# Attention and token/channel mixer on one core: the last tokens of all batches as a ninth batch, seeded banks, heads in pairs, order from a table

## The chip, the cores and the metric

The kernel runs on one core of a Trainium2 chip. The core has TensorE (PE; its weight loads are PEld), VectorE (DVE), ScalarE (ACT), GpSimd (POOL) and SyncE (SP). The metric is the device time of one execution in microseconds, smaller is better; all inputs start and the output ends in the chip's memory (HBM).

## What is computed

Eight batches, eight heads, 576 tokens, head width 64. Attention is causal by blocks of 64 tokens; its output, with the heads side by side (576 x 512 per batch), goes through a mixer over tokens and one over channels:

```python
scores = scale * np.matmul(q, k.transpose(0, 1, 3, 2))
scores = np.where(block_i >= block_j, scores, -1e9)
attn = softmax(scores)                      # over the keys
x = np.matmul(attn, v)                      # (8, 576, 512), heads side by side
h = np.maximum(xt @ w_tok1, 0.0) @ w_tok2   # xt: tokens last; 576 -> 256 -> 576
u = x + h.transpose(0, 2, 1)
h2 = np.maximum(u @ w_ch1, 0.0) @ w_ch2     # 512 -> 1536 -> 512
return u + h2
```

Inputs and output are float32; inside, operands of matmuls are bfloat16 and sums are float32.

## The kernel before

**Stages of one batch.** Q and K of four heads at a time (a group) are loaded on POOL's queue into `raws` and turned by DVE into `turned` (`load_qk`, L410; transposes L448). Scores are made in three sets per group (`score_set`, L550, matmuls L572), ACT takes the exponentials (L590), and per head ten matmuls multiply by V, whose 65th column of ones gives the sums (`head_out`, L607, matmuls L618). DVE takes the reciprocals (L638) and multiplies into `x_sb` (L644). The last 64 tokens of each batch (576 = 4 x 128 + 64) go apart: `ends_out` (L655, matmuls L671). The token mixer is `token_up` (L804) and the products L910 in `token_mix` (L883); `u` is turned into `uT` by a DMA transpose (L977).

**Channel mixer.** 512 tokens of each batch, and the last 64 tokens of two batches packed into 128 rows ("mixed", made at L941 to L972 for every odd batch). Up is 512 to 1536 channels with relu, down 1536 to 512 plus `u`.
- Batches 0 to 3: `channel_up` (L1028), 48 matmuls of 512 columns.
- Batches 4 and 5, and 6 and 7, in pairs: `channel_up_fast` (L1100), one Strassen step in Winograd's form: 12 channel blocks in 6 groups per pair, seven products of two matmuls of 512 columns in each. Three intermediate products are copied out of their bank to SBUF (`keep`), three results are added up from bank and copy (`join`), and relu is applied afterwards (`clip`).
- Down: batch 0 plainly; batches 1 to 7 by `channel_down_fast` (L1223), one Strassen step per batch, seven products of 12 matmuls of 256 columns (L1265), each followed by a `fold` on DVE into `o_sb` (L1288). Batch 7 goes in two half passes.
- Mixed rows: `channel_up_mixed` (L1053, 48 matmuls of 128 columns, L1063, three relus) and `channel_down(mixed=True)` (L1322, 12 matmuls of 512 columns, L1356, one fold), four times.

**Banks.** The sums lie in eight PSUM banks of 512 columns: two pairs `sc` for scores, four `mm` for everything else; after the last scores the pairs become four more single banks, `late`.

**Order.** Each operation is added to a plan with its engines, an estimated cost, its dependencies and a priority (`Plan.add`, L46). `Plan.run` (L99) plays the plan through with these costs: whenever an engine is free it takes the ready operation of lowest priority number, and that gives the order in which the instructions of each engine stand in its queue; it also picks DVE or ACT for operations that may go on either (`EVAC`). `Plan.search(1000)` (L70) repeats this with priorities moved at random and keeps the best. Engines execute their queues in order.

**Buffers.** Q/K three slots, output `o_sb` four, `sums` (operands of the down pass) five. The sums of the up weights (`up_weight_sums`, L1086) lie in the memory of `raws` and are made when the loads of Q and K are over.

**Start.** Before the first scores PE runs 16 warm-up matmuls (L378) and fillers of 256 columns (L385) in its holes up to 20 us.

Of the kernel before, what the change touches and what calls it, by code (L numbers as in the profile page):

```python
# [12 lines left out]
FP32 = mybir.dt.float32  # L13
BF16 = mybir.dt.bfloat16
# [17 lines left out]
class Plan:  # L32
# [5 lines left out]
    FIRST = {"POOL": 2.2, "ACT": 0.7, "SP": 0.7}  # L38
    def __init__(self):
        self.ops = []  # L40
        self.free = {}
# [18 lines left out]

    def fits(self, o, coming=()):
# [8 lines left out]
    def search(self, tries):  # L70

        prios = [o.prio for o in self.ops]
        modes = [o.mode for o in self.ops]
        slots = {name: list(free) for name, free in self.free.items()}

        def run(prios):
            for o, prio, mode in zip(self.ops, prios, modes):
                o.prio, o.mode = prio, mode
            self.free = {name: list(free) for name, free in slots.items()}
            try:  # L80
                order = self.run()
            except ValueError:
                return math.inf, ()
            return max(o.end for o in order if not o.quick), order

        rnd = random.Random(0)
        movable = [n for n, prio in enumerate(prios) if abs(prio) < 4e3]
        best = run(prios)[0]
        for _ in range(tries):
            moved = list(prios)  # L90
            count, width = rnd.choice((1, 2, 4, 8, 30, 100)), rnd.choice((0.3, 1, 3, 10))
            for n in rnd.sample(movable, count):
                moved[n] += rnd.uniform(-width, width)
            end = run(moved)[0]
            if end <= best:
                best, prios = end, moved
        return run(prios)[1]

    def run(self):  # L99
        for o in self.ops:  # L100
            o.users = []
            need = {}
            for pools, _ in o.take:
                need[pools] = need.get(pools, 0) + 1
            o.need = list(need.items())
# [15 lines left out]
        while left:  # L121
# [13 lines left out]
            for e in ("PE", "ACT", "DVE", "POOL", "SP"):  # L135
# [33 lines left out]
                o.end = busy[e] = t + o.cost[e]  # L169
# [7 lines left out]
                if o.xfer is not None:  # L177
                    first = o.end + self.FIRST[e]
                    if e == "POOL":
                        soft = max(soft, first) + o.xfer  # L180
                    else:
                        hard = max(hard, first) + o.xfer
                    o.end, lag = (soft if e == "POOL" else hard), 1.3
# [1321 lines left out]
```

## Time and profile before

| | us |
|---|---|
| median of three runs (lowest, highest) | 292.37 (291.93, 293.22) |
| the profiled execution | 292.19 |
| its span, first to last instruction | 290.4 |
| busy PE, DVE, ACT, POOL | 282.6, 229.2, 164.2, 62.5 |

The span is what the trace shows; 1.8 us of the execution's own time lie around it. Busy times are the union of an engine's instructions; on PE a matmul's time holds its drain, which overlaps the next, so what a matmul costs PE is read from start to start. "L1265" is line 1265 of the kernel. The chain is the work that ended last, followed back from the end.

### The profile page before, as it was taken

Reading aid. Unit: us, or ns where it says so; the run is one execution under the profiler, and the core shown is the slowest. Engines: PE = TensorE matmul, PEld = TensorE weight load, DVE = VectorE, ACT = ScalarE, POOL = GpSimd, SP = SyncE. Lnnn points to the kernel's source line nnn. Section 1 sums busy time; section 2 is a strip of 40 time slices with the busy share of each in tenths; the row PEclk is TensorE's granted clock in tenths of the full one; section 3 lists DMA queues with packets and bytes.
Section 4 is the critical chain, followed back from the end, with each engine's and each line's share of the span. In section 5 each row is a group of like instructions: output and inputs, shape, how many; then the busy total and the mean of one; then the engine's idle time right before and its main releaser. Section 6 shows DMA issues by size and latency. Waiting matters only on the chain.

```text
span 290.4 us, 9160 instructions
## 1 busy us (share of the span) xinstructions
PE 282.6 (97%) x3970; PEld 186.8 (64%) x3993; DVE 229.2 (79%) x496; ACT 164.2 (57%) x220; POOL 62.5 (22%) x101
## 2 busy tenths in 40 slices
PE   8999999998999999999999999999999999999995
PEld 3676456566647876646777576774447876466884
DVE  3765468887768988878999765978799958988983
ACT  5895984477767556767656787610587004665000
POOL 9765545541330061160050000000000000000000
PEclk9999999999999999999999999999999999999998
DMA  8999999999693099994386100611100903112053
GB/s 232 213 161 208 208 186 188 236 208 175 101 119 76 5 171 199 176 152 69 75 57 109 68 2 2 93 71 75 37 2 8 153 3 111 72 72 74 1 184 144
DMA packets 64840, 32.67 MB, mean 112 GB/s; under 512 B 53152, under 2 KB 55328, under 8 KB 64800
## 3 DMA queue, kind: packets, MB, share of 16 engines
q0 software_dynamic: 44032, 16.75, 49.4%
q1 hardware_dynamic: 20768, 15.34, 19.7%
q8 instruction: 31, 0.51, 0.7%
q14 instruction: 9, 0.07, 0.1%
HBM read 35.85 MB, written 9.44 MB: 156 GB/s over the span
## 4 chain that ended last, share of the span: by engine, by line
PE 88%; DMA 6%; POOL 3%; issue 1%; DVE 1%; ACT 0%; POOLq 0%
PE mm L1265 20%; PE mm L1036 15%; PE sc L572 9%; PE late L1141 6%; PE mm L1141 6%; PE mm L1356 6%; PE mm L618 6%; PE mm L813 4%; PE mm L910 4%; PE mm L1063 4%; DMA raws<-in_q_dram 3%; DMA vals<-in_v_dram 2%; PE late L1265 2%; PE mm L671 2%; PE mm L817 1%; POOL vals L474 1%
## 5 line engine op out<-in xcount | busy, mean ns | idle before, releaser
L590 ACT ACTIVATE e_sb<-sc 128x1024 bf16<-128x1024 f32 x95 | 92.3, 1023 | 34.9 <-PE sc L572 32.3
L448 DVE STREAM_TRANSPOSE turned<-raws 128x288 int32<-128x288 int32 (+1 forms) x65 | 41.0, 698 | 11.7 <-ACT raws L406 3.8
L1036 PE MATMUL mm<-uT,wc_sb 128*128 128x512 bf16 x192 | 46.0, 381 | 0.0
L474 POOL DMA_DIRECT2D vals<-in_v_dram x45 | 36.9, 835 | 37.0 <-PE mm L671 22.5
L572 PE MATMUL sc<-turned 32*64 32x64 bf16 (+7 forms) x1260 | 34.8, 293 | 1.3 <-ACT gT L799 1.0
L1036 PEld LDWEIGHTS <-wc_sb 128*128 128x128 bf16 x192 | 20.0, 115 | 18.3 <-issue 2.6
L572 PEld LDWEIGHTS <-turned 32*64 32x64 bf16 x1280 | 19.6, 104 | 14.5 <-issue 11.0
L1265 PEld LDWEIGHTS <-sums 128*128 128x128 bf16 x252 | 24.3, 98 | 3.5 <-DVE vals L598 0.4
L644 DVE TENSOR_TENSOR x_sb<-mm,rinv 128x256 bf16<-128x256 f32 x63 | 25.3, 420 | 1.0
L618 PEld LDWEIGHTS <-e_sb 128*128 128x128 bf16 x640 | 23.0, 97 | 4.3 <-issue 1.2
L1265 PEld LDWEIGHTS <-gT 128*128 128x128 bf16 x240 | 22.7, 98 | 4.6 <-issue 1.1
L618 PE MATMUL mm<-vals,e_sb 128*128 128x65 bf16 x630 | 25.4, 193 | 0.3 <-issue 0.2
L801 DVE TENSOR_SCALAR gT<-mm 128x512 bf16<-128x512 f32 x19 | 13.1, 688 | 10.9 <-PE mm L1036 10.8
L799 ACT ACTIVATE gT<-mm 128x512 bf16<-128x512 f32 x31 | 18.4, 601 | 4.5 <-PE mm L1036 4.2
L1288 DVE TENSOR_TENSOR o_sb<-mm,u_sb 128x512 f32<-128x512 f32 x23 | 15.8, 688 | 5.7 <-PE mm L1265 5.3
L1265 PE MATMUL mm<-wd_sb,sums 128*128 128x256 bf16 x150 | 18.4, 273 | 0.0
L813 PE MATMUL mm<-x_sb,w_sb 128*128 128x512 bf16 (+1 forms) x82 | 16.6, 317 | 0.3
L799 ACT ACTIVATE aT<-mm 128x512 bf16<-128x512 f32 (+1 forms) x16 | 8.7, 544 | 13.2 <-PE mm L817 12.9
L1141 PEld LDWEIGHTS <-raws 128*128 128x128 bf16 x96 | 9.3, 98 | 10.4 <-issue 0.5
L799 ACT ACTIVATE gmT<-mm 128x512 bf16<-128x512 f32 x9 | 5.4, 596 | 18.6 <-PE mm L1063 18.6
L425 POOL DMA_DIRECT2D raws<-in_k_dram x14 | 7.8, 554 | 36.3 <-DVE turned L448 32.1
L638 DVE RECIPROCAL rinv<-mm 128x4 f32<-128x4 f32 x63 | 10.1, 175 | 6.2 <-PE mm L618 5.5
(150 smaller groups left out, 491.8 us busy)
## 6 DMA issues: line engine op xcount, KB each, us to landing
out_dram<-o_sb SPq DMA_DIRECT2D x14, 512.0 KB, 2.8
raws<-in_k_dram POOLq DMA_DIRECT2D x14, 288.0 KB, 8.4
raws<-in_q_dram POOLq DMA_DIRECT2D x14, 288.0 KB, 7.7
vals<-in_v_dram POOLq DMA_DIRECT2D x28, 128.0 KB, 6.4
wc_sb<-in_moe_w_ch_dram POOLq DMA_DIRECT2D x8, 192.0 KB, 7.9
wc_sb<-in_moe_w_ch_dram POOLq DMA_DIRECT2D x3, 512.0 KB, 11.1
out_dram<-o_sb SPq DMA_DIRECT2D x10, 128.0 KB, 2.5
gT<-in_k_dram SPq DMA_DIRECT2D x4, 288.0 KB, 3.8
```

What stands on the lines that cost most here:

```text
L448: nc.vector.transpose(dst[:, 0:S, :] .rearrange("p s e -> p (s e)") .bitcast(I32) .rearrange("p (a k) -> p k a", k=NB)[:, k0:k1], raw2.bit ...
L474: nc.gpsimd.dma_start(out=t[128 - p : 128, J, hs, 0:64], in_=src)
L572: nc.tensor.matmul(out=home(n)[64 * half : 64 * half + 64, c : c + w], lhsT=bar[r, 0] if j is None else kT[i][r, 64 * j : 64 * j + 64, par ...
L590: nc.scalar.activation(dst, sc[SC.index(note["pool"])][:, :, 0:n], EXP, scale=scale)
L618: nc.tensor.matmul(out=u[:, I, 0:65], lhsT=e[:, h, c : c + 128], rhs=vt[:, J, head, 0:65], start=(J == 0), stop=(J == I),)
L644: nc.vector.tensor_tensor(out=xt[:, 0:4, 64 * head : 64 * head + 64], in0=u[:, :, 0:64], in1=ri[:, 0:4].to_broadcast([128, 4, 64]), op=MULT,)
L799: nc.scalar.activation(dst, src, RELU)
L813: nc.tensor.matmul(out=ps, lhsT=w1_sb[:, c, tt : tt + 255 : 2], rhs=xt[:, c, cols], start=(c == 0), stop=False)
L1036: nc.tensor.matmul(out=bank_of(bank), lhsT=wc1_sb[:, m, channels(cc)], rhs=uT[b % 2][:, :, m, :], start=(m == 0), stop=(m == NDM - 1),)
L1141: nc.tensor.matmul(out=bank_of(bank), lhsT=x(m), rhs=y[:, :, m, :], start=first and m == 0, stop=m == 1, skip_group_check=not first,)
L1265: nc.tensor.matmul(out=bank_of(bank)[:, 256 * i : 256 * i + 256], lhsT=x[:, kk, 128 * i : 128 * i + 128], rhs=y[:, kk], start=first and i ...
L1356: nc.tensor.matmul(out=ps, lhsT=gt[:, cc, c0 : c0 + 128], rhs=wc2_sb[:, cc, cols], start=(cc == 0 and not turned), stop=(cc == NDC - 1),)
```

## The change

The last 64 tokens of all eight batches are kept until batch 7 and form a ninth batch (number 8) of 512 rows: `um_sb` and `umT` now hold four pairs. Its up is the new `channel_up_half`, a Strassen step within one batch (halves of the tokens take the place of two batches), three groups of seven products of four matmuls of 256 columns; its down is `channel_down_fast`. The mixed functions go.

In `channel_up_fast`, `channel_up_half` and `channel_down_fast` the running sum is copied from its bank into another bank (`seed`), onto which further matmuls accumulate, in place of a copy to SBUF or a fold. A bank that was not filled whole by its last matmuls gets one matmul over all its columns first (`cover`); the plan keeps such banks apart (pools `full` and `late` against `mm` and `late mm`) and counts 0.22 us for it.

Two heads take two banks and are normalised by one reciprocal and one multiply (`pair_out`). Q/K buffers fall from three to two slots, `o_sb` from four to three, `sums` from five to three. `ws_sb` gets memory of its own, and the sums of the up weights are added to the plan at batch 1. Copies and clears of the tails may go to POOL. The random trials go: each operation's priority is shifted by an entry of a table (`SHIFTS`), and a second table (`ONLY`) fixes the engine of some. The plan still orders the operations.

```diff
+    def bare(self, note):
+        return note.get("seed", False) and note["pool"] in ("mm", "late mm")
...
+    def placed(self):
+        letters = {"A": "ACT", "D": "DVE", "P": "POOL"}
+        shifts, only = [int(x) for x in SHIFTS.split()], "".join(ONLY.split())
+        for o, shift, letter in zip(self.ops, shifts, only):
+            o.prio += 0.05 * shift
+            if letter in letters:
+                o.engines = (letters[letter],)
+        return self.run()
...
-                o.end = busy[e] = t + o.cost[e]
+                o.end = busy[e] = t + o.cost[e] + 0.22 * sum(self.bare(note) for _, note in o.take)
...
-    sums = ring(5, [128, NDC // 2, 256], BF16, "sums")
-    o_sb = ring(4, [128, 2, DM], FP32, "o_sb")
+    sums = ring(3, [128, NDC // 2, 256], BF16, "sums")
+    o_sb = ring(3, [128, 2, DM], FP32, "o_sb")
...
+    EARLY = ("mm", "full")
+    BANK = ("mm", "late mm", "full", "late")
+    SEED = ("full", "late", "mm", "late mm")
     WARM, KEEP = 16, 110
-    FAST_UP = 4
+    HALF_UP, FAST_UP = 4, 4
...
+    def cover(bank):
+        if P.bare(bank):
+            nc.tensor.matmul(out=bank_of(bank), lhsT=ident, rhs=wc1_sb[:, 0, 0:512], start=True, stop=True)
...
-        i = (2 * b + hg) % 3
+        i = (2 * b + hg) % QK
...
+    def pair_out(b, pair, deps, prio, urgent=0):
...
+        banks = [{"covers": False}, {"covers": False}]
...
+                    take=() if avs or av else [(EARLY, x) for x in banks], urgent=urgent,
...
+        rc = P.add("DVE", 0.2, emit_rc, avs + reuse(key), prio - 1, urgent=urgent)
...
+        mu = P.add("DVE", dve_cost(512), emit_mu, [rc], prio - 1, give=banks, urgent=urgent)
...
+    def channel_up_half(b, uT_done, wc1_ready, prio):
+        t = [th_sb[:, 0], th_sb[:, 1], ut[:, 2:4, 0:2, :], th_sb[:, 2]]
+        b11, b12, b21, b22 = (ut[:, 2 * n : 2 * n + 2, j : j + 2, :] for j in (0, 2) for n in range(2))
...
+        for n, dst, x, y in ((0, t[0], b12, b11), (1, t[1], b22, t[0]), (2, t[2], b22, b12), (3, t[3], b21, t[1])):
+                nc.vector.tensor_tensor(out=dst, in0=x, in1=y, op=SUB)
...
+        for k in range(NDC // 4):
+            banks = {to: {"covers": True, "seed": to in "cd"} for to in "aecd"}
...
+            base = uT_done + wc1
+            op = product(0, "a", a_of(0, 0), b11, base)
+            r1 = keep(product(1, "e", s_of(0), t[0], [made[0], op] + ws_ready))
+            seed("c", op)
+            seed("d", product(3, "a", s_of(1), t[1], [made[1]] + ws_ready))
+            final(0, 0, "c", product(2, "c", a_of(0, 1), b21, base))
+            r7 = join(0, 1, "d", [product(4, "d", s_of(3), b22, base + ws_ready), r1], True)
+            r3 = join(1, 1, "a", [product(5, "a", s_of(2), t[2], [made[2]] + ws_ready), r1], False)
+            clip(0, 2, 1, [r7, r3])
+            final(1, 0, "a", product(6, "a", a_of(1, 1), t[3], [made[3]] + wc1))
...
-            r1 = keep(0, "a", product(0, "a", a_of(0, 0), b11, base))
-            r6 = keep(1, "e", product(1, "e", s_of(0), t[0], [made[0]] + ws_ready))
-            r2 = keep(2, "a", product(3, "a", s_of(1), t[1], [made[1]] + ws_ready))
-            r5 = join(0, c1, 0, "c", [product(2, "c", a_of(0, 1), b21, base), r1], True)
-            clip(0, slice(c1, c1 + 1), [r5])
-            r7 = join(1, c1, 2, "e", [product(4, "e", s_of(3), b22, base + ws_ready), r2], True)
-            r3 = join(1, c2, 1, "a", [product(5, "a", s_of(2), t[2], [made[2]] + ws_ready), r6], False)
+            op = product(0, "a", a_of(0, 0), b11, base)
+            r1 = keep(product(1, "e", s_of(0), t[0], [made[0], op] + ws_ready))
+            seed("c", op)
+            seed("d", product(3, "a", s_of(1), t[1], [made[1]] + ws_ready))
+            final(0, c1, "c", product(2, "c", a_of(0, 1), b21, base))
+            r7 = join(1, c1, "d", [product(4, "d", s_of(3), b22, base + ws_ready), r1], True)
+            r3 = join(1, c2, "a", [product(5, "a", s_of(2), t[2], [made[2]] + ws_ready), r1], False)
...
-            fold("a", 0, 0, product(0, "a", a11, b11), True, False)
+            op = product(0, "a", a11, b11)
+            def emit(o, nt=nt, banks=banks):
+                src, dst = (bank_of(banks[to])[:, 0 : 256 * nt] for to in "ac")
+                cast(o, dst, src)
+            last["a"] = last["c"] = P.add(EVAC, evac_cost(256 * nt), emit, [op], prio - 1)
+            fold("c", 0, 0, product(0.5, "c", a12, b21), True, True)
...
-            fold("c", 0, 0, product(5, "c", a12, b21), False, True)
...
-            if p % 2 == 1:
-                gm_done = channel_up_mixed(p // 2, um_done, wc1_ready, 10 * p + 3.5)
-                channel_down(p, gm_done, wc2_ready, um_rows, prio, mixed=True)
+            if p == B - 1:
+                gm_done = channel_up_half(B, um_all, wc1_ready, MIXED[0])
+                channel_down_fast(B, gm_done, wc2_ready, um_rows_all, MIXED[1])
...
-        for op in P.search(1000):
+        for op in P.placed():
             op.emit(op)
```

## The prediction

> **What bounds the kernel now.** I read the page's busy shares first, then the chain, then busy time by stage, then the chain piece by piece where the changed products run, then the waits of TensorE (PE). Span 290.4 us; this execution took 292.19 us in all, 0.18 us under the median of 292.37.
>
> The page's shares and the chain by engine:
>
> ```profile
> PE 282.6 (97%) x3970; PEld 186.8 (64%) x3993; DVE 229.2 (79%) x496; ACT 164.2 (57%) x220; POOL 62.5 (22%) x101
> ...
> PE 88%; DMA 6%; POOL 3%; issue 1%; DVE 1%; ACT 0%; POOLq 0%
> ```
>
> PE works 97% of the span and carries 88% of the chain. A share is an average, so the stages (each row: window, span, then busy PE, PEld, DVE, ACT, POOL):
>
> ```profile
> 0.00:13.50 13.50, 12.30 (x146) 6.58 (x147) 7.57 (x20) 9.33 (x14) 11.13 (x26) 1.00 1.21 230
> 13.50:27.00 13.50, 13.20 (x284) 9.82 (x281) 8.46 (x32) 10.74 (x16) 8.27 (x16) 1.00 1.16 177
> 27.00:70.00 43.00, 41.19 (x699) 24.84 (x712) 32.03 (x77) 29.37 (x38) 20.08 (x30) 1.00 1.45 205
> 70.00:150.00 80.00, 79.43 (x1423) 51.98 (x1428) 65.74 (x155) 53.73 (x65) 21.89 (x31) 1.00 0.84 109
> 150.00:200.00 50.00, 49.84 (x803) 34.45 (x805) 40.66 (x92) 27.98 (x35) 1.12 (x2) 1.00 0.36 67
> 200.00:282.00 82.00, 81.76 (x595) 54.99 (x597) 71.26 (x118) 33.05 (x54) 0.00 (x0) 1.00 0.24 60
> 282.00:290.40 8.40, 4.91 (x46) 4.16 (x43) 3.53 (x9) 0.00 (x0) 0.00 (x0) 0.91 0.44 159
> ```
>
> PE is without work for 0.30 + 1.81 + 0.57 + 0.16 + 0.24 = 3.1 us between 13.5 and 282 us, at full clock. Before 13.5 us its busy time is mostly the warm-up and filler matmuls (L378, L385); there the chain is loading, 3.73 to 10.94 us for the first V. The last 8.4 us hold the last products and the last store. So from 13.5 us on, time changes with PE's work, plus or minus those 3.1 us, as long as DVE (87% in the last long stage) and the banks keep up.
>
> What PE pays per product, from the chain (start, us until the next piece, what):
>
> ```profile
> 180.55 0.89 PE mm L1063 x16
> ...
> 239.59 1.31 PE mm L1265 x12
> ...
> 242.23 0.86 PE late L1141 x4
> ```
>
> So a 128-column matmul costs 0.89/16 = 56 ns of PE, a 256-column one 1.31/12 = 109 ns, a 512-column one 0.86/4 = 215 ns. The mean durations of the groups (219, 273, 379 ns) hold the drain, which overlaps the next matmul; I don't use them for PE.
>
> **Ninth batch (PE).** Removed: four times the mixed up (48 matmuls of 128 columns) and the mixed down (12 of 512): 192 x 56 ns = 10.7 us and 48 x 215 ns = 10.3 us, together 21.1. Added: `channel_up_half` for batch 8 alone (`HALF_UP` equals `FAST_UP`, so no other batch takes it): 3 x 7 products of 4 matmuls of 256 columns, 84; `channel_down_fast(8)`: 7 products of 12, 84. 168 x 109 ns = 18.3 us. Net -2.7 us, on the path since PE has no slack. (Columns fall from 24576 to 21504 in up and in down alike, by 1/8.)
>
> [...]
>
> **Seeds and covers (PE).** A seed is a copy from one bank to another onto which matmuls then accumulate. Seeds: 2 in each of 12 groups of the two fast pairs, 2 in each of 3 groups of the ninth up, one per down pass (batches 1 to 6, two half passes of 7, the ninth): 24 + 6 + 9 = 39. Where the bank was not last filled whole by matmuls, `cover` issues one 128x512 matmul first, 215 ns. Bounds: none, 0; all, 39 x 0.215 = 8.4 us. Most users of a bank fill it whole (ups, token products); those that don't are head pairs, ends, PE transposes and the half passes of batch 7, and a seed takes a filled bank first. After 200 us no heads are left and four of the eight banks start out filled by scores. A seeded product waits for its copy (588 ns on ACT) as the product on bank a waited for a keep before; the queue behind it on PE is then product 1 or another group, so I add nothing. I take 4 covers, near the low end, for the three early down passes and the half passes: +0.9 us. [...]
>
> **Fewer, larger operations on DVE and ACT.** Heads: 64 reciprocals (175 ns) and 64 multiplies of 128x256 (420) become 32 and 32; a 128x8 reciprocal by the rows 128x2 and 128x4 (166, 175) is about 193, a 128x512 multiply by the other 128x512 reads of a bank 688: 38.1 to 28.2, -9.9 us DVE. Fast pairs: each of 12 groups loses one join (685, DVE) and one 512-wide clip, two of three keeps become seeds, one relu is added: -8.2 us DVE, about +7 on either engine, less 12 clips of 288 (DVE) or 630 (ACT). Down passes: of 7 folds (689) one becomes a copy: -4.8 DVE, +4.2 on either (ACT's copy is 588). Ninth batch: DVE gains 4 sums of 1536 (955), 4 of 512 (between 0 and the 553 of 768; I take 420), 6 joins, 6 folds and loses 4 folds: 3.8 + 1.7 + 4.1 + 4.1 - 2.8 = +10.9; 16 copies and relus and 3 clips replace 12 relus, about +4. Sum: DVE -12 of 229 us, ACT about +10 of 164. Neither bounds; cost on the path 0, covered by PE. If that cover is gone, it is in the stage after 200 us, where the ninth batch's +10.9 and -8.2 -2.1 for folds meet 71 of 82 us: about even, 87% again.
>
> **Order, by the table.** What it can win on PE is the 3.1 us of holes. The longest is at 68.5 us, where a score set waits for ACT:
>
> ```profile
> PE sc L572 <- ACT gT L799: 1.0, 1, 1.0
> PE mm L1356 <- issue: 0.3, 2, 0.2
> PE sc L572 <- DVE turned L448: 0.3, 1, 0.3
> ```
>
> It is a late slot in a queue, not a lack of engine time: ACT is busy 29 of 43 us from 27 to 70, where most of the holes lie, and DVE 32; there DVE gets 1.2 us a batch back from the heads (9.9/8). Bounds: -3.1 (all closed) to +3 (as many again, since the banks below are tighter). I take -2.0, nearer the closed end because the last 212 us already show what a good order reaches: 0.97 us of holes. The filler at the start (29 matmuls of 109 ns, 3.2 us) stands for waits on loads and exps; ACT is busy 9.3 of the first 13.5 us. I count nothing there, with -1.5 to +1 for the range.
>
> **Moved or narrowed, counted as nothing.** Sums of the up weights go from the last stage to batch 1 (4 x 0.95 us of DVE, whose idle share in 27 to 70 us is 25%). Clears and copies of tails may go to POOL (22% busy; but its queue also issues the V and Q/K loads, so one late copy delays them; the load then lands after its 8 us). Q/K buffers 3 to 2: POOL's issue now waits for the transposes of two groups ago, not three. The lead is there: the last Q/K loads go out at 127 us and are transposed at 154. The queue behind such a wait holds the V loads. Output ring 4 to 3, sums 5 to 3: a down pass (84 x 109 = 9.2 us) frees its first sum after two products; a store lands in 2.8 us. Before, DVE waited once, 1.3 us, for a store; I expect a few such waits on DVE, and PE has the other bank's products meanwhile. Eight 128 KB stores of the last tokens become four of 256 KB on SP's queue. Tail unchanged: 3.5 us from the last matmul to the end.
>
> **Sum.** 292.19 - 2.74 + 0.86 - 2.0 = 288.3; with 0.18 to the median and rounding, 288.4.
>
> **Rivals.**
> *The table also fills the start.* All holes closed (-3.1), two covers (+0.4), 1.5 us less filler: 292.4 - 2.7 + 0.4 - 3.1 - 1.5 = 285.5. For it: the start is the one stretch where PE does work that isn't needed. Against: its chain is loads.
> *Covers eat the gain.* 15 covers are 3.2 us; with half the holes closed, 292.4 - 2.7 + 3.2 - 1.5 = 291.4, no difference. For it: with four banks during attention, heads leave them unfilled again and again. Against: 30 of the 39 seeds can run after attention.
> *Bank waits (slower).* While heads run there are four banks beside the score banks. A head pair takes two at once and keeps both from its first product to the end of a 688 ns multiply, about 2 x 0.3 + 0.2 + 0.19 + 0.2 + 0.69 = 1.9 us, where a head kept one for about 1.3; a down pass now holds c from its first product. PE executes in order, so every late bank is a hole. At 0.25 us per pair, 28 pairs of batches 1 to 7, that is 7 us: 292.4 - 2.7 + 0.9 + 7 = 297.6; it decides from 0.13 us per pair on (3.7 us, which uses up the 2.7 and the order's 2.0 less covers). For it: DVE, which frees the banks, is 82% busy in 70 to 150. Against: PE's waits in that stage are 0.57 us in all, none for a head's multiply.
> *That nothing changes on PE* would need the ninth batch not to replace the mixed products; the loop adds it in their place, so it isn't given a chance.
>
> **How the numbers follow.** My case 0.55, with its own range 286.5 to 290.8; start filled 0.17; covers 0.15; bank waits 0.13. A difference under 0.5% (1.5 us) is about what a measurement of this kernel can't tell from none. Faster: 0.53 + 0.17 + 0.02 (few covers) = 0.72; same: 0.02 + 0.12 + 0.02 (mild bank waits) = 0.16; slower: 0.11 + 0.01 = 0.12. The range leaves out the best twentieth of the start case and most of the bank case: 284.8 to 293.5.
>
> **What would show it.** PE's start to start 109 ns in the ninth batch and 168 matmuls there; the count of 128x512 matmuls reading `ident` and the up weights gives the covers (4 expected); PE's holes between 13.5 us and the last product about 1 us; reciprocals and multiplies at 32 each, 0.19 and 0.69 us; DVE's busy time near 217 us, ACT's near 174. The prediction is wrong if PE waits for the heads' multiplies, if more than about 10 covers appear, or if the stage after the last scores shows PE waiting for DVE's sums and joins.

## The result, and the profile after

| | before | after |
|---|---|---|
| median, us (lowest, highest; runs) | 292.39 (beside it on the same chip) | 487.43 (484.12, 488.36; 4) |
| ratio, 95% interval | | 1.664 [1.659, 1.669] |
| span of the profiled execution, us | 290.4 | 486.6 |
| busy PE, DVE, ACT, POOL, us | 282.6, 229.2, 164.2, 62.5 | 343.8, 239.0, 160.1, 67.7 |
| granted PE clock (share of full speed), mean over the span | 0.997 | 0.884 |

The change costs 195 us where 4 us of gain were forecast. First the page of after, in the order in which the page of before was read: busy shares, PE's busy tenths and its clock in 40 slices, the chain by engine, and the two groups of the head pairs.

```profile
PE 343.8 (71%) x3919; PEld 207.0 (43%) x3919; DVE 239.0 (49%) x437; ACT 160.1 (33%) x210; POOL 67.7 (14%) x117
...
PE   8777586577656766666766777685576788775995
...
PEclk9959999857999976895899775779989999998899
...
PE 59%; DVE 26%; ACT 9%; issue 4%; DMA 1%; DVEq 0%; ACTq 0%; SPq 0%
...
L740 DVE RECIPROCAL rinv<-mm 128x8 f32<-128x8 f32 x32 | 6.6, 207 | 44.0 <-PE mm L713 14.8
L747 DVE TENSOR_TENSOR x_sb<-mm,rinv 128x512 bf16<-128x512 f32 x32 | 22.1, 691 | 7.1 <-PE mm L1461 2.6
```

No engine is the bound any more: PE works 71% of the span, DVE 49%, ACT 33%. PE's share of the chain falls from 88% to 59%, and DVE (26%) and ACT (9%) now stand in it. The loss is even: nearly every slice shows PE at 5 to 8 tenths, but for two near the end at 9. PE's idle time is 486.6 - 343.8 = 142.8 us (7.8 before).

The stages (window, span, busy PE, PEld, DVE, ACT, POOL, granted clock, DMA share, GB/s), three of eleven, say the same:

```profile
0.00:30.00 30.00, 23.09 (x383) 15.06 (x384) 15.06 (x41) 16.47 (x21) 21.83 (x47) 0.94 1.19 196
...
100.00:150.00 50.00, 32.89 (x476) 17.66 (x473) 21.99 (x44) 18.05 (x23) 8.33 (x14) 0.85 0.44 53
...
450.00:486.60 36.60, 30.87 (x261) 26.12 (x259) 25.43 (x44) 2.45 (x5) 0.00 (x0) 0.96 0.28 87
```

What takes PE's place is read in the chain, piece by piece (start, us until the next piece, what), in the middle of attention:

```profile
128.24 0.70 DVE aT L903
...
128.99 1.04 PE mm L1134 x4
...
130.05 0.61 ACT aT L901
...
130.68 0.70 DVE gT L903
...
131.42 1.04 PE mm L1010 x4
...
132.48 0.70 DVE u_sb L1025
...
133.23 1.04 PE mm L1010 x4
...
134.29 0.70 DVE u_sb L1025
...
135.03 1.04 PE mm L1134 x4
```

Each line begins as the one before ends, but for 0.02 to 0.05 us. PE makes one product into one bank, stops, DVE or ACT empties one bank (an evacuation), stops, and PE makes the next. Before, four matmuls of 512 columns cost PE 0.86 us and the evacuations (588 to 690 ns) ran beside the next product; here a product and one evacuation take 1.04 + 0.70 + 0.07 = 1.81 us. And what a product waits for need not be anything it reads. The timeline of the same stretch (start, us, engine, line, what, in brackets the idle time before and what ended it):

```profile
131.42 1.02 PE L1010 MATMUL mm<-aT,w_sb 128*128 128x512 bf16 x4 [0.80 <-DVE gT L903]
...
133.23 1.02 PE L1010 MATMUL mm<-aT,w_sb 128*128 128x512 bf16 x4 [0.78 <-DVE u_sb L1025]
...
139.25 1.02 PE L1134 MATMUL mm<-uT,wc_sb 128*128 128x512 bf16 x4 [0.78 <-DVE gT L903]
```

The token mixer's down product (L1010) reads `aT`, and starts when DVE has put the relu of the channel mixer into `gT`; the channel mixer's up product (L1134) reads `uT` and waits for a `gT` that only a later stage needs. What they have in common with those evacuations is the tile `mm`.

Only the four `mm` banks are so. The other four (`late`, after the last scores) are separate tiles, and on them the same products run with next to no pause. By shape, groups of PE (busy us, mean ns, then idle time before them and what ended it):

```profile
L1461 PE MATMUL mm<-wd_sb,sums 128*128 128x256 bf16 x114 | 15.4, 288 | 4.2 <-DVE x_sb L747 2.6 <-DVE gT L903 0.8 <-ACT aT L901 0.7
L1461 PE MATMUL late<-wd_sb,sums 128*128 128x256 bf16 x78 | 9.5, 272 | 0.7 <-ACT mm L498 0.7
L1461 PE MATMUL late<-wd_sb,gT 128*128 128x256 bf16 x48 | 5.9, 273 | 0.0
```

And in the chain near the end there is a piece `459.76 7.86 PE late L1461 x72`: 72 matmuls of 256 columns at 109 ns without a hole, the price that the prediction used. The `late` banks are in use only after the scores, so time and tile change together here; e1 and e2 below part them.

The diff shown further up leaves out the lines that do this. In the kernel before the four banks are four tiles, `mm = ring(4, [128, 512], FP32, "mm", psum)`. In the changed kernel they are one tile of four banks, cut into views, so that a pair of heads in two banks can be read by one instruction (`both`, in `pair_out`):

```diff
-    mm = ring(4, [128, 512], FP32, "mm", psum)
+    mm_all = psum.tile([128, 4, 512], FP32, name="mm")
+    mm = [mm_all[:, i] for i in range(4)]
```

### The profile page after: what moved, and what is told of

The parts are those of the page before. It is cut to its first block, busy times and chain, and to the rows that moved or that the text cites. A ratio compares the mean times of both kernels' runs of the same rounds, so it can differ in the third digit from the quotient of the medians.

```text
span 486.6 us, 8972 instructions
## 1 busy us (share of the span) xinstructions
PE 343.8 (71%) x3919; PEld 207.0 (43%) x3919; DVE 239.0 (49%) x437; ACT 160.1 (33%) x210; POOL 67.7 (14%) x117
## 3 DMA queue, kind: packets, MB, share of 16 engines
q1 hardware_dynamic: 20704, 15.34, 11.3%
## 4 chain that ended last, share of the span: by engine, by line
PE 59%; DVE 26%; ACT 9%; issue 4%; DMA 1%; DVEq 0%; ACTq 0%; SPq 0%
PE mm L1134 12%; PE mm L1461 11%; PE mm L713 6%; DVE x_sb L747 4%; PE mm L1327 4%; PE late L1461 4%; PE mm L1010 4%; DVE o_sb L1485 4%; ACT gT L901 4%; PE mm L915 4%; DVE gT L903 3%; DVE u_sb L1025 3%; PE mm L1556 2%; PE sc L664 2%; PE mm L776 2%
## 5 line engine op out<-in xcount | busy, mean ns | idle before, releaser
L1134 PE MATMUL mm<-uT,wc_sb 128*128 128x512 bf16 x192 | 58.8, 444 | 24.4 <-ACT gT L901 5.7
L1134 PEld LDWEIGHTS <-wc_sb 128*128 128x128 bf16 x192 | 22.5, 121 | 53.5 <-issue 43.6
L540 DVE STREAM_TRANSPOSE qk_sb<-qk_sb 128x288 int32<-128x288 int32 (+1 forms) x65 | 41.7, 697 | 5.1 <-ACT qk_sb L498 3.5
L664 PE MATMUL sc<-qk_sb 32*64 32x64 bf16 (+7 forms) x1260 | 38.9, 325 | 0.2 <-ACT e_sb L682 0.2
L1461 PEld LDWEIGHTS <-sums 128*128 128x128 bf16 x288 | 29.1, 101 | 15.7 <-issue 10.1
L1461 PEld LDWEIGHTS <-gT 128*128 128x128 bf16 x288 | 28.9, 102 | 11.8 <-issue 7.3
L1025 DVE TENSOR_TENSOR u_sb<-mm,x_sb 128x512 bf16<-128x512 f32 x23 | 15.4, 689 | 28.9 <-PE mm L1010 12.5
L664 PEld LDWEIGHTS <-qk_sb 32*64 32x64 bf16 x1280 | 20.7, 112 | 18.4 <-issue 14.7
L1010 PE MATMUL mm<-aT,w_sb 128*128 128x512 bf16 x54 | 19.9, 483 | 12.0 <-DVE u_sb L1025 5.9
L740 DVE RECIPROCAL rinv<-mm 128x8 f32<-128x8 f32 x32 | 6.6, 207 | 44.0 <-PE mm L713 14.8
L747 DVE TENSOR_TENSOR x_sb<-mm,rinv 128x512 bf16<-128x512 f32 x32 | 22.1, 691 | 7.1 <-PE mm L1461 2.6
L517 POOL DMA_DIRECT2D qk_sb<-in_q_dram x14 | 7.7, 550 | 89.8 <-DVE qk_sb L540 87.8
L1327 PEld LDWEIGHTS <-ws_sb 128*128 128x128 bf16 x96 | 9.5, 100 | 22.4 <-issue 11.8
L1461 PE MATMUL mm<-wd_sb,sums 128*128 128x256 bf16 x114 | 15.4, 288 | 4.2 <-DVE x_sb L747 2.6
## 6 DMA issues: line engine op xcount, KB each, us to landing
wc_sb<-in_moe_w_ch_dram POOLq DMA_DIRECT2D x3, 512.0 KB, 11.3
```

What stands on the lines that cost most here:

```text
L540: nc.vector.transpose(dst[:, 0:S, :] .rearrange("p s e -> p (s e)") .bitcast(I32) .rearrange("p (a k) -> p k a", k=NB)[:, k0:k1], raw2.bit ...
L664: nc.tensor.matmul(out=home(n)[64 * half : 64 * half + 64, c : c + w], lhsT=bar[r, 0] if j is None else kT[i][r, 64 * j : 64 * j + 64, par ...
L747: nc.vector.tensor_tensor(out=dst[:, ::-1] if flip else dst, in0=both(0, 64), in1=ri.to_broadcast([128, 2, 4, 64]), op=MULT,)
L1010: nc.tensor.matmul(out=bank_of(bank), lhsT=w2_sb[:, t, 128 * si : 128 * si + 128], rhs=at[:, t, :], start=(t == 0), stop=(t == NDT - 1),)
L1134: nc.tensor.matmul(out=bank_of(bank), lhsT=wc1_sb[:, m, channels(cc)], rhs=uT[b % 2][:, :, m, :], start=(m == 0), stop=(m == NDM - 1),)
L1461: nc.tensor.matmul(out=bank_of(bank)[:, 256 * i : 256 * i + 256], lhsT=x[:, kk, 128 * i : 128 * i + 128], rhs=y[:, kk], start=first and i ...
```

## The experiments

Four theories were put on record over the runs. **A**: with one tile over four banks, an operation on one of them waits for the last accesses of other engines to any of the four. **B**: the table's order is bad for the chip. **C**: the joint instruction on two banks holds PE up. **D**: only a tile of four banks is treated so, narrower ones are not. Later, on what is left of the change: **R**, that refills of PE's instructions come late behind loads, against **V** (V or Q/K data come late) and **O** (order or banks).

**e1: after, with four tiles again.** The heads are then normalised singly, by two reciprocals and two multiplies, since the joint access (`both`) is a view of one tile. The order in every queue is that of after.

```diff
-    mm_all = psum.tile([128, 4, 512], FP32, name="mm")
-    mm = [mm_all[:, i] for i in range(4)]
+    mm = ring(4, [128, 512], FP32, "mm", psum)
...
-            nc.vector.reciprocal(ri, both(64, 65))
+            for i in range(2):
+                nc.vector.reciprocal(ri[:, i], one(i, 64, 65))
...
-            nc.vector.tensor_tensor(
-                out=dst[:, ::-1] if flip else dst,
-                in0=both(0, 64),
-                in1=ri.to_broadcast([128, 2, 4, 64]),
-                op=MULT,
-            )
+            for i in range(2):
+                nc.vector.tensor_tensor(
+                    out=dst[:, i], in0=one(i, 0, 64), in1=ri[:, i].to_broadcast([128, 4, 64]), op=MULT
+                )
```

> The changed kernel with its four banks `mm` as four tiles again, as in the kernel before; the two heads of a pair are therefore normalised by two reciprocals and two multiplies (a joint access needs one tile). The order of every engine's queue is the changed kernel's. Theory A (the one tile over four banks: an operation on one of its banks is made to wait for the last operation of another engine on the other banks, so PE, DVE and ACT take turns): the holes close, 285 to 293 us, DVE about 10 us busier than 239. Theory B (the table's order is bad, each queue standing behind the wrong operation): order unchanged, so 470 to 490 us. Theory C (the joint read of two banks by one DVE operation is what holds PE): also 285 to 293; told from A by the run e3.

Measured: 290.4 us (289.59 to 292.31, five runs), before 292.2; ratio 0.9925 [0.9907, 0.9944]. The time lies where A and C put it; DVE is 4 us less busy than in after (234.6 against 239.0), where A expected 10 more. The profiled execution is the slowest of the five (292.31, span 290.5). So 197 of 487 us go with three lines, and the rest of the change is worth 0.75%. Its page and stages:

```profile
PE 279.2 (96%) x3898; PEld 188.7 (65%) x3919; DVE 234.6 (81%) x501; ACT 158.5 (55%) x210; POOL 67.8 (23%) x117
...
PE 93%; DMA 1%; issue 1%; ACT 1%; DVE 1%; SPq 0%; ACTq 0%
```

```profile
13.50:27.00 13.50, 10.95 (x277) 8.51 (x278) 9.04 (x34) 6.83 (x9) 9.63 (x18) 0.91 1.20 177
27.00:70.00 43.00, 42.37 (x705) 25.68 (x698) 31.55 (x74) 29.54 (x38) 18.44 (x27) 0.99 1.33 181
70.00:150.00 80.00, 79.53 (x1413) 52.72 (x1419) 70.34 (x160) 50.93 (x60) 24.36 (x40) 1.00 0.91 121
150.00:200.00 50.00, 49.74 (x740) 31.58 (x744) 39.34 (x92) 28.85 (x39) 5.14 (x7) 1.00 0.44 67
200.00:282.00 82.00, 82.00 (x616) 61.45 (x615) 73.50 (x120) 33.25 (x55) 0.00 (x0) 1.00 0.20 59
```

From 27 us on PE is without work for 0.63 + 0.47 + 0.26 + 0.00 = 1.36 us (2.78 before). Against it stands one stretch, 13.5 to 27 us: 2.55 us of holes (0.30 before), and the granted clock is 0.91. It comes back below.

The extra 196.1 us of span in after against e1 split into 131.5 us of more PE idle time (142.8 against 290.5 - 279.2 = 11.3) and 64.6 us of more PE busy time (343.8 against 279.2): a product with a pause behind it takes longer (four matmuls of 512 columns 1.04 us of the chain, where before had 0.86), and the granted clock is lower (0.884 against 0.989 in the profiled execution of e1); the shares of these two were not parted.

**e2: the kernel before, with one tile.** Nothing else; the order on PE, DVE and ACT is that of before.

```diff
-    mm = ring(4, [128, 512], FP32, "mm", psum)
+    mm_all = psum.tile([128, 4, 512], FP32, name="mm")
+    mm = [mm_all[:, i] for i in range(4)]
```

> The kernel before with one edit: its four banks `mm` are slices of one tile of 128x4x512 in place of four tiles. Order, operations and buffers are those of the kernel before. Theory A: 420 to 520 us, the same taking of turns. Theories B and C: 292 us, nothing changes.

Measured: 504.3 us (501.5, 507.1), ratio 1.73 [1.71, 1.74]. The waits have the same face (engine, line, waited for: us in total, times, longest): a product of the heads waits for a fold of the channel mixer, a product of the channel mixer for a multiply of the heads.

```profile
PE mm L619 <- DVE o_sb L1289: 5.7, 6, 1.8
...
PE mm L1037 <- DVE x_sb L645: 4.7, 6, 0.9
```

The tile alone, without table, pairs, seeds or ninth batch, does all of it. B is gone as the cause of the loss.

**e3: after, one tile kept, heads normalised singly.** It parts the joint instruction from the tile.

```diff
-            nc.vector.reciprocal(ri, both(64, 65))
+            for i in range(2):
+                nc.vector.reciprocal(ri[:, i], one(i, 64, 65))
...
-            nc.vector.tensor_tensor(
-                out=dst[:, ::-1] if flip else dst,
...
+                nc.vector.tensor_tensor(
+                    out=dst[:, i], in0=one(i, 0, 64), in1=ri[:, i].to_broadcast([128, 4, 64]), op=MULT
```

> The changed kernel with its one tile, but heads normalised one by one (two reciprocals, two multiplies). Theory A: 480 to 510 us, as slow as the changed kernel or a little slower. Theory C: 285 to 300 us. Theory B: 480 to 500.

Measured: 481.5 us (one run), 6 us below after. Page:

```profile
PE 331.4 (69%) x3898; PEld 204.5 (43%) x3919; DVE 241.4 (50%) x501; ACT 160.0 (33%) x210; POOL 67.8 (14%) x117
...
PE 57%; DVE 28%; ACT 9%; issue 5%; DMA 1%; another core or an unknown queue 0%; DVEq 0%; ACTq 0%; SPq 0%
```

C falls: the 32 joint reads have next to nothing to do with it. They are only the reason why the tile was made.

**e6: the kernel before, with two tiles of two banks.**

```diff
-    mm = ring(4, [128, 512], FP32, "mm", psum)
+    mm_two = ring(2, [128, 2, 512], FP32, "mm", psum)
+    mm = [mm_two[i // 2][:, i % 2] for i in range(4)]
```

> The kernel before with its four banks `mm` as two tiles of two banks each. Theory A (an access to one bank of a tile waits for the last accesses to all its banks): in between, 340 to 440 us, since half of the other users of a bank's tile are gone; by PE's waits on DVE that ask for the last or last but one DVE instruction (25% in the kernel before, 92% with one tile, 66% here) a straight line gives 292 + 0.61 x 212 = 422. Theory D (only a tile of more banks than the score tiles' two is treated so): 292 to 296.

Measured: 336.3 us (336.07, 336.56), ratio 1.151 [1.147, 1.155]. D falls: it would be no different from before. A has the kind right but not the size: 336.3 is just under its range (340 to 440) and far under the 422 of its straight line, so the time doesn't grow in step with the share of such waits. PE's waits, and the stage with the most attention:

```profile
PE mm L619 <- DVE x_sb L645: 3.4, 5, 1.2
PE mm L619 <- ACT gT L800: 3.2, 4, 0.8
PE mm L1266 <- DVE o_sb L1289: 1.9, 5, 1.0
```

```profile
70.00:150.00 80.00, 70.63 (x1228) 45.83 (x1229) 56.71 (x136) 47.87 (x60) 19.14 (x27) 1.00 0.90 116
```

Heads' products (L619) wait for a relu of the channel mixer (`gT`), which shares only the tile with them. The program of each kernel shows it without a run. Of PE's waits on DVE, the share that asks for the last or the last but one DVE instruction that stands ahead of it in the program, and the same for ACT:

```
                          PE's waits on DVE   on ACT   time, us
before, four tiles               25%            63%     292.4
before, two tiles (e6)           66%            84%     336.3
before, one tile (e2)            92%            99%     504.3
after, four tiles (e1)           31%            81%     290.4
after, one tile                  85%            98%     487.4
```

In the kernel before, PE's wait on DVE asks, in the median, for an instruction that is followed by three later ones, so that DVE may be late by three; with one tile (e2) it asks for the last one. By these counts, about one operation in flight is what is left of concurrency on these banks. That is theory A, shown by adding the tile (e2), taking it away (e1) and halving it (e6). That accesses are put in order by tile, and not by the bank or the columns of a view, is what these programs show; a wait of the chip itself for another bank was not seen.

**What the rest of the change is worth: e4, e5, e10.** e4 is e1 without its table; e5 replaces the table by the 1000 random trials of the kernel before; e10 keeps the table and runs such trials from its priorities.

```diff
         shifts, only = [int(x) for x in SHIFTS.split()], "".join(ONLY.split())
+        shifts, only = [0] * len(shifts), "." * len(only)
```

> Run e1 with all shifts of the table zero and no engine fixed by it: the plan orders by its own priorities. Theory A: between 295 and 315 us, since the plain order leaves some holes on PE; the table is then worth 5 to 25 us. Theory B: faster than e1, since the bad order is gone.

e5 has that line and the search of the kernel before; e10 has the search alone, on the table's priorities:

```diff
-        return self.run()
...
+        best = run(prios)[0]
+        for _ in range(1000):
+            moved = list(prios)
+            count, width = rnd.choice((1, 2, 4, 8, 30, 100)), rnd.choice((0.3, 1, 3, 10))
+            for n in rnd.sample(movable, count):
+                moved[n] += rnd.uniform(-width, width)
+            end = run(moved)[0]
+            if end <= best:
+                best, prios = end, moved
+        return run(prios)[1]
```

> Run e1 without the table, but with the kernel before's own way to an order: 1000 random trials from the plain priorities. It compares the two kernels at the same effort for the order. If the ninth batch, the seeds and the pairs are worth 2.7 us of PE by themselves: 289 to 291. If the gain of e1 is the table's alone: 292 to 296 (e4, without trials, has 296.8).

> e1 with its table, its costs unchanged, and 1000 random trials started from the table's priorities, kept by the plan's costs. If what the table is worth lies in what the plan's costs can see, the trials find a like order or a better one: 289 to 291.5 us. If the table fits what the plan can't see (refills, the real landing of loads), orders that look better to the plan are worse on the chip: 292 to 297 us.

Measured: e4 296.84 us (296.0, 297.69), ratio 1.016 [1.012, 1.019]. e5 299.15 us (295.29 to 300.05, four runs), ratio 1.019 [1.012, 1.027]. e10 290.97 us, ratio 0.994 [0.992, 0.996]; three of its four runs lie within 0.2% (290.52 to 291.03), and the fourth, the profiled one, took 979.9 us with matmuls of 512 columns at a mean of 1085 ns instead of 381 ns and a granted clock of 1.00 in the records, for which nothing here gives a cause; nothing else is read from it.

So without a table the new structure, with 2.7 us less for PE, is 4.6 us slower than the old, and the table is worth 6.4 us (296.8 against 290.4). e5's median lies above both of its ranges (289 to 291 and 292 to 296; one of its four runs is in the second): orders that the plan's costs favour show no gain on the chip when the trials start from the plain priorities. Trials from the table neither help nor harm. A seventh kernel (e7), with costs for two single multiplies in place of one joint one and trials from the table, ran for 3.15 us and holds none of the work: with these costs the plan finds no order from the table and returns an empty one, so it says nothing of the question.

```diff
-        rc = P.add("DVE", 0.2, emit_rc, avs + reuse(key), prio - 1, urgent=urgent)
+        rc = P.add("DVE", 0.36, emit_rc, avs + reuse(key), prio - 1, urgent=urgent)
...
-        mu = P.add("DVE", dve_cost(512), emit_mu, [rc], prio - 1, give=banks, urgent=urgent)
+        mu = P.add("DVE", 2 * dve_cost(256), emit_mu, [rc], prio - 1, give=banks, urgent=urgent)
```

> Run e1 with the table as the start of 1000 further trials and with the costs of the split normalisation put right in the plan (0.36 and twice a 128x256 read, for 0.2 and one of 128x512). Theory A with the order's holes as what is left: 287.5 to 290, below e1's 290.4 by up to 2. If e1's holes come from what the plan doesn't know: 290 to 292.

**Where e4's time goes: late instructions.** The stage from 70 to 150 us of e4 has 3.5 us of holes and a clock of 0.98:

```profile
70.00:150.00 80.00, 76.49 (x1359) 49.57 (x1363) 60.59 (x145) 53.81 (x65) 24.25 (x38) 0.98 0.98 109
```

The first reading was that V lands late: both holes stand at products that read V. The timeline of e4 (start, us, engine, line, what; in brackets the idle time and what ended it) says otherwise:

```profile
111.35 0.29 PE L713 MATMUL mm<-vals,e_sb 128*128 128x65 bf16 x4
...
113.09 0.66 PE L713 MATMUL mm<-vals,e_sb 128*128 128x65 bf16 x16 [1.45 <-issue]
...
119.25 0.26 PE L773 MATMUL mm<-vals,e_sb 128*64 128x65 bf16 x5
...
121.30 0.23 PE L773 MATMUL mm<-vals,e_sb 128*64 128x65 bf16 x3 [1.79 <-issue]
```

The holes lie inside a run of products, after 4 of 20 and after 5 of 8, and in the program the instruction behind each waits for no semaphore (from semaphore events the profile infers which engine released which). Between the two stand exactly 256 of PE's instructions. The page of every kernel has a queue of its own for instructions, here e1's (queue, packets, MB, share):

```profile
q8 instruction: 30, 0.49, 0.7%
```

That is 30 packets of 16 KB. PE has 7847 instructions in the program; if these packets carry them, it is some 260 to a packet, which fits the 256 counted. In the traces of before and after, whose packets on q8 hold 16384 bytes each, PE goes through 254 and 253 instructions of its program, in the mean, from the start of one packet to the start of the next. In the trace's packets each such hole follows one:

```
kernel   packet on q8 (us)   hole ends   from the packet's end   hole, us
e1        21.11 -  22.05       23.54            1.49               2.2
e4       110.64 - 111.59      113.09            1.50               1.45
e4       118.69 - 119.78      121.30            1.52               1.79
e5       111.47 - 112.42      113.72            1.30               1.62
e5       121.48 - 123.58      125.13            1.55               4.98
e9       111.35 - 112.30      113.77            1.47               1.00
e9       121.30 - 122.28      123.91            1.63               3.70
```

(The rows of e5 and e9 are from the slowest execution of each, 300.05 and 298.18 us; those of e4 from the faster of its two.) The reading, theory R, is that PE had run out of instructions. The place of the holes fits it: numbered in the programs' lists of PE's instructions, the first one behind the hole is number 3775 or 4031 in e4, e5 and e9, and number 703 in e1. 4031 - 3775 is 256, and 3775 - 703 is 12 x 256. (In e1 the weight load behind the hole waits for nothing; the matmul behind it waits for ACT, which was done at 21.49.) Counted in blocks of 256 from these places, in e4 a packet begins within 1.7 us of PE's entry into the block before it from 130 to 190 us, but 2.1 to 3.7 us after it before 70 us and 5.3 to 5.6 us after it from 110 to 125 us; the worst is 7.8 us (e5, second hole). A block of attention is executed in 4 to 13 us.

What the packets are late beside is DMA traffic, not loads alone. In e1 from 15 to 24 us it is POOL's loads (eight issues from 15.84 to 21.41 us; 177 GB/s from 13.5 to 27 us). In e4 from 108 to 123 us most of the packets' time is on SP's queue (q1: one output store, transposes of `u`) and less on POOL's (q0: Q and K); queue, packets, MB, share:

```profile
q1 hardware_dynamic: 2741, 1.14, 81.7%
q0 software_dynamic: 909, 0.82, 47.6%
```

e8 and e9 put R on trial. e8 cuts the loads of Q and K from batch 3 on to a quarter; e9 moves the loads of V earlier.

```diff
-                def emit_load(o, hbm=hbm, raw2=raw2):
-                    nc.gpsimd.dma_start(out=raw2, in_=hbm)
+                def emit_load(o, hbm=hbm, raw2=raw2, w=288 if b >= 3 else 1152):
+                    nc.gpsimd.dma_start(out=raw2[:, 0:w], in_=hbm[:, 0:w])
```

> The version without the table (e4), with every Q and K load of batches 3 to 7 cut to its first 288 of 1152 columns; the rest of each buffer keeps older values, so the output isn't the reference's. Order of every queue, every wait and every instruction's size are unchanged but for these loads. Theory R: the two holes of e4 on PE (1.45 us ending at 113.1, 1.79 us ending at 121.3 us) are refills of PE's instructions that came late behind loads: both stand 256 instructions apart inside a group of products, no semaphore is waited for, and each ends 1.5 us after a 16 KB packet of the instruction queue. With the loads cut both holes close: 292.8 to 294.3 us (296.8 less 3.2 is 293.6, a little more or less for the rest). Theory V: PE waits there for V or Q/K data; then too the time falls, but the holes that stay stand before the first product of a group, at a wait. Theory O: the holes belong to PE's order or to the banks: 296 to 298 us, both holes there.

```diff
-                prio = (10 * b + (0, 5.7, 6)[min(b, 2)] if b else (-95.5, 5.15)[hg]) + 0.01 * J
+                prio = (10 * b + (0, 2.7, 3)[min(b, 2)] if b else (-95.5, 5.15)[hg]) + 0.01 * J
```

> The version without the table (e4), with the priority of the V loads of batches 1 to 7 lowered by 3, so that POOL's queue issues the five V loads of a batch one to three loads of Q and K earlier; the order on PE differs in about 4% of its instructions. Theory V (V lands late behind Q and K): 293 to 295 us, the holes at 113 and 121 us gone. Theory R (late refills of instructions behind any loads): the same bytes are moved at other times, so the holes move with the traffic and the time stays at 295 to 298 us, with holes inside groups of products that end 1.3 to 1.6 us after a packet of the instruction queue.

Measured: e8 289.79 us (289.69 to 290.61, four runs), ratio 0.991 [0.989, 0.993], 7 us under e4; no hole of PE over 0.2 us without a releaser is left, and the stage reads

```profile
70.00:150.00 80.00, 79.73 (x1428) 52.53 (x1437) 63.78 (x151) 56.73 (x69) 27.10 (x41) 1.00 0.79 83
```

That is below R's range: it gains more than the 3.2 us of the two holes. Of the 6.2 us between the two spans (293.8, 287.6), the clock, 1.00 instead of 0.98 in that stage, makes by estimate another 1.6 (0.02 x 80, as if the time went with the clock), and the last 1.4 were not followed. e9 gives 296.34 us over ten runs, ratio 1.008 [1.004, 1.012], but they fall in two groups: four of 292.95 to 294.65 us at a clock of 0.999 to 1.000, and six of 295.81 to 298.18 us at 0.993 to 0.994. The first group lies in V's range (293 to 295) but for 0.05 us, the second in R's (295 to 298) but for 0.2, so the time doesn't part them. The trace does, for one execution, the slowest of the ten (298.18): the largest wait of PE without a releaser and the second are again in a run of products,

```profile
PE mm L773 <- issue: 3.7, 1, 3.7
...
PE mm L713 <- issue: 1.0, 1, 1.0
```

256 instructions apart and at the same two numbers of PE's stream as in e4 and e5. So where the holes show, they aren't waits for V: V as the cause of them falls, R stands. That earlier V loads make them rarer is possible and not shown; the faster group left no trace. e8's shorter loads may also land sooner (no row here has it), which alone could not tell R from V; the holes without a wait, the 256 and e9's trace do. e8 shows that taking bytes of Q and K away closes the holes (none over 0.2 us without a releaser is left); whether fewer transposes or another time of the store would do it too was not run. How a packet is held up (behind which transfers, for how long) no view shows.

What is still a guess is why e1, with the table, mostly escapes. Its order may spread refills and loads another way; its one such hole (21.5 to 23.5 us, L944, in the chain below) is in the profiled execution, the slowest of five; the other four have spans of 287.8 to 289.4 us.

```profile
21.10 0.39 ACT aT L897
21.49 2.04 issue
23.54 0.40 PE mm L944 x4
```

**The best version.** e1 is a little faster than the kernel before: 290.4 us, ratio 0.9925 [0.9907, 0.9944].

## Why the prediction was wrong

Forecast 288.4, measured 487.4; "faster" had 0.72, "slower" 0.12. By its steps:

**The step that failed: what the banks cost.** The sum counted bank waits at nothing, and the seeds' wait with them ("the queue behind it on PE is then product 1 or another group, so I add nothing"). That other products go on while one bank is emptied holds for four tiles (PE idle for 7.8 us in before); for one it does not (142.8 us in after). The nearest rival, bank waits, had half of it right: "PE executes in order, so every late bank is a hole" (in the trace of before all 3993 weight loads of PE start in the order of the program), and it decides "from 0.13 us per pair on". But it took the wait from how long a head pair holds two banks, on 28 pairs, 7 us in all; e3 shows that the pairs are not the cause (481.5 us with single heads), and e2 and e1 that each evacuation of any of the four banks is (+212 and +197 us). The lines of the change that make one tile of four appear nowhere in the prediction, in no term, rival or sign of being wrong, and "against" was argued from PE's waits in the kernel before, where the tiles were four. A bound from both sides for "does a view of a shared tile still count as a bank of its own?" would have had all evacuations in a row with PE as the dear case: in the trace of before 381 instructions of DVE and ACT read an `mm` bank, 183 us in sum, and with PE's 283 us that is an estimate of 466 us (measured 504.3 in e2). It was not made.

**Ninth batch, -2.74: right.** In e1 the 84 matmuls of its up (L1199) take 9.2 us of the chain, 110 ns each; its down matmuls share line and form with those of the other batches, of which 72 in one piece take 7.86 us in after and in e1, 109 ns each. So the spacing of 109 ns at 256 columns held in these pieces, and at 512 columns, where the prediction had 215 ns, ten matmuls in one piece of e1 (L1323) take 2.16 us, 216 ns each.

**Covers, +0.86: none needed.** In after and e1 no matmul stands on the cover's line, and the built programs have none. Each seed finds a bank that a product has filled. The lower bound (0) was the truth; 4 was a guess above it. What a cover is needed for, no run shows.

**Order, -2.0: -1.4 after 27 us, and then lost again in part.** Holes fall from 2.78 to 1.36 us. In the profiled run of e1, 2.25 us of holes come in from 13.5 to 27 us, and a clock of 0.91 there and 0.99 up to 70 us costs, by estimate (as if the time went with the clock), another 13.5 x 0.09 + 43 x 0.01 = 1.6. The terms add up: -2.7 - 1.4 + 2.25 + 1.6 = -0.3, and its span against that of before is +0.1. In the four other runs of e1 the span is 1.0 to 2.6 us under before's 290.4. So the change without the one tile would have been forecast at 288.4 with a span of 286.6, and took 290.4: right in sign, about half in size. The "start filled" rival lost by the same stretch: the start did not fill, it got worse.

**Moved, "counted as nothing": what the new traffic does to PE's refills.** The prediction saw that two Q/K slots make POOL's queue wait and hold the V loads behind it. What was found is another place: by theory R, PE's own refills come late beside bunched traffic (holes of 1.0 to 5.0 us). e4 and e5, without the table, take 296.8 and 299.2 us; with a quarter of the late Q/K bytes e8 takes 289.8. Whether the third slot's loss is what bunches the traffic stays open: no run gives the slot back. What was put down to order (holes that a better queue closes) is thus in part the luck of when transfers and refills meet, as e9's two groups suggest.

**DVE and ACT.** Forecast 217 and 174 us for joint heads; after has 239.0 and 160.1. The pairs' own durations were right (forecast 193 and 688 ns, measured 207 and 691). Their gain was mis-sized: 64 multiplies of mean 413 ns keep DVE busy for 23.8 us in e1, not 26.4, as back to back they overlap; with reciprocals 32.7 us single against 28.7 joint, 4.0 us where 9.9 were taken from means times counts. And the table gives DVE more of the evacuations that either engine may do: e1 has 234.6 and 158.5, e4 without it 224.6 and 170.0. Neither matters while PE bounds.

```profile
L746 DVE TENSOR_TENSOR x_sb<-mm,rinv 128x256 bf16<-128x256 f32 x64 | 23.8, 413 | 0.1
```

**What it had named as proof.** "PE waits for the heads' multiplies" came true in after, but as one of many. The costliest group of PE, with its idle time and what ended most of it:

```profile
L1134 PE MATMUL mm<-uT,wc_sb 128*128 128x512 bf16 x192 | 58.8, 444 | 24.4 <-ACT gT L901 5.7 <-DVE x_sb L747 5.6 <-DVE u_sb L1025 4.9
```

Relus, heads and the token mixer's sums share the blame alike. No covers. After the last scores PE does wait for DVE's joins in after (L1327 for `gT` of L1360: 1.7 us); in e1 it doesn't (82.00 us busy of 82 from 200 us on).

## What to carry to other kernels

Before anything else in a diff, read the lines that change what a buffer is: four tiles merged into one and cut into views shared their waits here, and with engines that took turns on the four banks that was worth more than any instruction saved (1.7 times the time for 4 us of DVE). Count, in the built program, how far behind each wait reaches: where 85 to 99% of PE's waits asked for the last instruction of the other engine or the one before it (after, e2), next to nothing overlapped; at 66% on DVE and 84% on ACT (e6) the time was 15% longer. When PE stops inside a run of products with no semaphore, look at the instruction queue's packets before suspecting data, and number the instructions: the holes here lay a multiple of 256 apart and ended 1.3 to 1.6 us after a packet of that queue.

## What the runs showed of the hardware that was not expected

- One of the DMA queues moves instructions: 31 packets of 16 KB in before and 30 in after and e1, and from one to the next PE goes through 253 to 254 instructions in the mean (before, after). Beside other transfers PE stood still for 1.0 to 5.0 us, waiting for nothing that the profile shows, at places a multiple of 256 instructions apart, and went on 1.3 to 1.6 us after such a packet's end (e1, e4, e5, e9). That these holes are refills that came late is theory R's reading.
- The granted clock was lower in many stages with holes of PE, but not by PE's busy share alone: in after it is 0.79 to 0.85 from 100 to 350 us, where PE is busy 66 to 69% of the time, but 0.93 at 69% (60 to 100 us) and 0.96 to 0.97 at 72 to 73% (350 to 450 us). It is 0.91 in the stretch with one hole of 2.2 us in e1, but 1.00 throughout e6, where PE is busy 88% from 70 to 150 us in many short holes (longest 1.2 us). What sets the clock, these runs do not show.
